# Filler products on TensorE and a reordered start in a state-space and ELU kernel

## The chip, the cores and the metric

The kernel runs on one core of a Trainium2 chip. The metric is device time in microseconds for one execution; before the change the median of seven runs is 390.37 us (389.13 to 390.76).

TensorE is PE in the profile (its weight loads PEld), VectorE DVE, ScalarE ACT, GpSimd POOL, and SyncE, which issues most transfers here, SP.

## The reference

A chunked linear recurrence (Mamba-2) is followed by a two-layer network with an ELU between the layers. All is float32.

```python
for c in range(nc):                       # per batch and head, chunks of the sequence
    cum = np.cumsum(log_a[chunk])         # log_a = log(clip(a, 1e-6, 1))
    M = (C @ B.T) * exp(cum_i - cum_j) * causal
    y = M @ x + (C @ state) * exp(cum)
    state = exp(cum_last) * state + sum_j exp(cum_last - cum_j) * outer(B_j, x_j)
h = y_transposed @ w_in                   # 3072 x 256 by 256 x 2048
g = where(h > 0, h, exp(min(h, 0)) - 1)
out = g @ w_out                           # 3072 x 2048 by 2048 x 256
```

There are 4 batches of 8 heads, a sequence of 768, head size 32 and state size 16. The weights come as 64-bit numbers, and the kernel makes 32-bit ones of them on the chip.

## The kernel before, in words

The sequence is cut into twelve chunks of 256 tokens (chunk `n`, of one batch and all heads). Each chunk has an attention part and then layer 1 and layer 2 of the network. The order of instructions on every engine is that of the program text; nothing is rescheduled. Each engine works its own queue in that order and waits where data or buffers are missing.

The attention part of a chunk is a chain of small products on TensorE with copies and products on the other engines between them:

- `turn` (L369) transposes B and C; ACT copies B out as `bt`, DVE masks C into `ctm` (L382).
- `first_exp` (L349), for the first chunks, spreads exp(cum) over the state rows: a product into `ps_ec`, copied by ACT to `ec`. `turn_exp` (L386) makes `cts` from it on DVE.
- `scaled` (L360) multiplies B by its decay on GpSimd, giving `sc`. `sums` (L481) multiplies `sc` by x into `ps_st`. `states` (L497) carries the state on DVE (`S_new`), and GpSimd masks it into `Sx`.
- `first_decays` (L424) takes four exps of 128x256 on ACT, giving L. `scores` (L451) makes `ps_g`, and `weigh` (L466) makes M = g times L on DVE, in four parts.
- `across` (L523) and `inside` (L543) sum the output in `ps_y`: `across` from the states, `inside` from M and x, in two halves `t`. The halves are copied to `yT`.

`l1(n, i)` (L578) is one of eight steps of layer 1 for a chunk: two groups of 128 hidden columns, each two products of 128x256 in f32, into `ps_h`. `elu` (L594) follows: two instructions on ACT (`e`), one on DVE (`g`). `l2` (L610) is the matching step of layer 2.

The weights come in sixteen pieces, eight of `w_in` and eight of `w_out`. A piece is loaded by `w_load` (on SP's queue), and converted by `w_abs` (ACT, L157), `w_low` (ACT or DVE, L164 or L166), `w_sign` (DVE, L174), `w_high_a` (DVE, the clip of `mag`, L182), `w_high_b` (DVE, L189) and `w_sum` (GpSimd, L199). Step `i` of layer 1 needs piece `i`.

The head of the program (L654 to L746) holds chunks 0 and 1 with the first four steps of layer 1. A first batch of seven idle products (L214, bf16 on zeros, 128x512) stands at the very start of TensorE's queue. The loop at L751 then goes through twelve layer-1 steps of chunks 0 and 1 and the attention of chunk 2. The main loop from L794 alternates one step of layer 2 of chunk n - 2 with one step of layer 1 of chunk n, and places the attention of later chunks between them. `ends` (L786) names the step at which `across` and `inside` of a pair of later chunks are put.

PSUM buffers come from two pools: seven rotating ones (`p_a`, tag `a`), handed out in the order in which they were released, and a single one (`p_o`, tag `o`).

Of the kernel before, what the change touches and what calls it, by code (L numbers as in the profile page):

```python
# [16 lines left out]
P = 128  # L17
# [11 lines left out]
def kernel(  # L29
# [49 lines left out]
    def psum(shape, name):  # L79
        return p_a.tile(shape, F32, tag="a", name=name)  # L80
# [70 lines left out]
    def w_words(i):  # L151
        words = w_raw[i].rearrange("p k (f t) -> p k f t", t=2)
        return words[:, :, :, 0], words[:, :, :, 1]
# [15 lines left out]

    w_sgn = {}  # L170

    def w_sign(i):
        w_sgn[i] = conv.tile([P, 2, CW], U32, tag="sgn", name="sgn")
        nc.vector.tensor_scalar(  # L174
            out=w_sgn[i], in0=w_words(i)[1], scalar1=0x80000000, scalar2=None,
            op0=ALU.bitwise_and)

    def w_high_a(i):
        mag = w_mag[i]


        nc.vector.tensor_scalar(  # L182
            out=mag.bitcast(F32), in0=mag.bitcast(F32),
            scalar1=high_word_as_f32(0x38000000), scalar2=high_word_as_f32(0x47EFFFFF),
            op0=ALU.max, op1=ALU.min)
# [26 lines left out]
    def idle_products(count):  # L212
        for _ in range(count):
            nc.tensor.matmul(  # L214
                out=ps_idle, lhsT=idle, rhs=idle.unsqueeze(1).to_broadcast([P, 4, P]),
                start=True, stop=True)

    idle_products(7)
    ident = const.tile([P, P], F32, name="ident")
# [36 lines left out]
    def make_heads(n):  # L256
# [5 lines left out]

    make_heads(0)
    make_heads(1)
    nc.gpsimd.tensor_scalar(
        out=la, in0=la, scalar1=1e-6, scalar2=1.0, op0=ALU.max, op1=ALU.min)


    def log_of(t):
        nc.scalar.activation(t, t, ACT.Ln)  # L270
# [7 lines left out]
    def to_last(cum, out, eng):  # L278
# [3 lines left out]
            out=out.rearrange("r u (v i) -> r (u v) i", i=Q),  # L282
            in0=cum[:, :, Q - 1:Q].to_broadcast(list(cum.shape)), in1=cum, op=ALU.subtract)

    nc.vector.tensor_scalar(
        out=la0, in0=la0, scalar1=1e-6, scalar2=1.0, op0=ALU.max, op1=ALU.min)
    log_of(la0)
    F0 = const.tile([P, 2, P], F32, name="F0")
    running_sums(la0, F0, P)
# [24 lines left out]
    def turned(src, name, scale, eng):  # L314
        rows = src.shape[0]
        ps = psum([P, 2, rows], "ps_" + name)
        for u in range(2):
            nc.tensor.transpose(out=ps[:, u], in_=src[:, u], identity=ident[0:rows, 0:rows])
        t = const.tile([P, 2, rows], F32, name=name)
        if eng is nc.scalar:  # L320
            eng.copy(out=t, in_=ps)
        else:
            eng.tensor_scalar(out=t, in0=ps, scalar1=scale, scalar2=None, op0=ALU.mult)
        return t
# [23 lines left out]

    def first_exp(n):  # L349

        ps = psum([P, 2, P], "ps_ec") if n else p_o.tile([P, 2, P], F32, tag="o", name="ps_ec")
        rows = slice(BH, 2 * BH) if n < 2 else slice(0, ROWS)
        nc.tensor.matmul(
            out=ps, lhsT=heads[n][rows].rearrange("p h n -> p (h n)"),
            rhs=X0 if n < 2 else F[:, 1], start=True, stop=True,
            tile_position=(rows.start, 0))
        st[n]["ec"] = att.tile([P, 2, P], F32, tag="ec", name="ec", bufs=4)
        nc.scalar.copy(out=st[n]["ec"], in_=ps)
# [10 lines left out]
    def turn(n):  # L369

        s = st[n]
        tb, tc_ = psum([P, 2, P], "ps_tb"), psum([P, 2, P], "ps_tc")
        for k, ps in enumerate((tb, tc_)):
            for u in range(2):
                nc.tensor.transpose(  # L375
                    out=ps[:, u], in_=s["bc"][:, k, u].rearrange("p h n -> p (h n)"),
                    identity=ident)
        s["bt"] = att.tile([P, 2, P], F32, tag="bt", name="bt", bufs=3)
        nc.scalar.copy(out=s["bt"], in_=tb)
        s["ct"] = tc_  # L380
        s["ctm"] = att.tile([P, 2, 2, P], F32, tag="ctm", name="ctm")
        nc.vector.tensor_tensor(  # L382
            out=s["ctm"], in0=tc_.unsqueeze(2).to_broadcast([P, 2, 2, P]),
            in1=hmask2.unsqueeze(1).unsqueeze(3).to_broadcast([P, 2, 2, P]), op=ALU.mult)
# [39 lines left out]
    def first_decays(n, *qs):  # L424

        s = st[n]
        if "L" not in s:
            s["L"] = att.tile([P, NH, 2, Q], F32, tag="L", name="L", bufs=4)
        for q in qs:
            nc.scalar.activation(s["L"][:, 2 * q:2 * q + 2], s["low"][q], ACT.Exp)  # L430
# [20 lines left out]
    def scores(*ns):  # L451

        gs = [psum([P, len(ns), 2, 2, Q], "ps_g") for _ in range(4)]
        for at, n in enumerate(ns):
            s = st[n]
            for u in range(2):
                for v in range(2):
                    for q in range(4):
                        rows, toks = slice(32 * q, 32 * q + 32), slice(Q * v, Q * v + Q)
                        nc.tensor.matmul(  # L460
                            out=gs[q][toks, at, u], lhsT=s["bt"][rows, u, toks],
                            rhs=s["ctm"][rows, u, :, toks], start=True, stop=True,
                            tile_position=(32 * q, Q * v), skip_group_check=True)
            s["g"], s["M"] = [g[:, at] for g in gs], []

    def weigh(n, q):  # L466
        s = st[n]
        M = att.tile([P, 2, 2, Q], F32, tag="M", name="M", bufs=8)
        nc.vector.tensor_tensor(  # L469
            out=M, in0=s["g"][q],  # L470
            in1=s["L"][:, 2 * q:2 * q + 2].rearrange("p k u i -> p u k i"), op=ALU.mult)
        s["M"].append(M)
# [70 lines left out]
    def inside(y, *ns):  # L543


        for t in range(2):
            for at, n in enumerate(ns):
                s = st[n]
                for u in range(2):
                    for v in range(2):  # L550
                        toks = slice(Q * v, Q * v + Q)
                        for q in range(4):
                            h, col = 4 * t + q, (D * q + shift(n, v)) % P
                            nc.tensor.matmul(  # L554
                                out=y[t][v][col:col + D, at, u],
                                lhsT=s["x"][toks, u, D * h:D * (h + 1)],
                                rhs=s["M"][h // 2][toks, u, h % 2], start=False, stop=True,
                                tile_position=(Q * v, col), skip_group_check=True)
            n = ns[0]
            if n // 2 not in yT:  # L560
                yT[n // 2] = ffn.tile([P, KC, 2, 2, P], F32, tag="yT", name="yT")
            out = yT[n // 2][:, t, n % 2:n % 2 + len(ns)]
            for v in range(2):
                k = shift(n, v)
                for at in (0, k) if k else (0,):
                    count, src = P - k, (at + k) % P
                    to, src = out[at:at + count, :, :, Q * v:Q * v + Q], y[t][v][src:src + count]
                    if t and n < 2:
                        nc.vector.tensor_copy(to, src)
                    else:  # L570
                        nc.scalar.copy(out=to, in_=src)  # L571
        for n in ns:
            st.pop(n)
# [88 lines left out]
    first_cum(0)  # L662
    first_decays(0, 0, 1)
    eb0 = turned(E0, "eb0", 1.0, nc.vector)
    turn(0)
    first_exp(0)
    scaled(0, nc.gpsimd)
    first_decays(0, 2, 3)
    turn_exp(0)
    sums(0, parts=(most,))  # L670
    states(0, most)
# [1 line left out]
    w_low(0, nc.scalar)  # L673
    log_of(la)
    scores(0)
    weigh(0, 0)
    weigh(0, 1)
    w_sign(0)
    w_high_a(0)
    w_high_b(0, half[0])  # L680
    w_sum(0, half[0])
    weigh(0, 2)
    weigh(0, 3)
    w_high_b(0, half[1])
    w_sum(0, half[1])
    w_abs(1)
    w_low(1, nc.scalar)
    kept = st[0]
    inside(across(0), 0)

    w_sign(1)
    w_high_a(1)
# [58 lines left out]
    for s, (n, i) in enumerate((  # L751
            (1, 0), (1, 1), (0, 4), (1, 2), (0, 5), (1, 3), (0, 6), (1, 4), (0, 7), (1, 5),
            (1, 6), (1, 7))):
        l1(n, i)
        if s < 8:
            decay_of(2, s)
        if s % 2 == 1 and todo < 10:
            w_take(todo, nc.vector)
            w_give(todo)
            w_load(todo + 6)  # L760
            todo += 1
        if s == 4:
            scaled(2, nc.gpsimd)
        if s == 5:
            turn(2)
            first_exp(2)
            turn_exp(2)
        if s == 7:
            scores(2)
            weigh(2, 0)  # L770
            weigh(2, 1)
        if s == 8:
            spread_cum(3)
            load_x(3)
            spread_exp(3)
            weigh(2, 2)
            weigh(2, 3)
            sums(2, pool=p_o, tag="o")
            states(2)
        if s == 10:  # L780
            inside(across(2), 2)
        if len(lag) > 1:
            elu()


    ends = {(3, 14): 4, (5, 8): 6, (7, 13): 8, (9, 7): 10}  # L786

    def end_of_two(n, step):
        m = ends.get((n, step))
# [101 lines left out]
```

## Time and profile before

| | |
|---|---|
| median of the runs | 390.37 us |
| the profiled execution | 390.84 us |
| its span | 389.0 us |
| mean granted clock of TensorE | 0.991 |
| PE busy | 379.9 us (98%) |
| DVE, ACT, POOL busy | 142.4, 196.5, 74.9 us |
| moved by DMA | 25.24 MB, mean 65 GB/s |
| layer 1 and layer 2 products in the chain that ended last | 41% and 44% of the span |

The page cuts the span into forty slices. Each digit is the busy share of a slice in tenths; the clock row gives the TensorE clock that was granted, in tenths of full speed. The timeline gives the start and the length of an instruction (or of several of one kind, merged, with their number), and in square brackets how long the engine had stood idle and what ended it. An f32 product on TensorE has two records.

### The profile page before, as it was taken

How to read it: one execution, taken by the hardware profiler on the slowest of the kernel's cores; microseconds unless marked ns; L12 is line 12 of the kernel's file. 1: busy time of each engine (PE TensorE's matmuls, PEld its weight loads, DVE VectorE, ACT ScalarE, POOL GpSimd, SP SyncE). 2: the span in 40 equal slices, each digit the busy share in tenths (PEclk: the TensorE clock that was granted, in tenths of full speed). 3: DMA queues.
4: the chain of work that ended last, by engine and by line, in shares of the span. 5: the costliest groups of instructions: out<-in, count | busy, mean ns of one | idle time of the engine just before them, and what ended most of it. 6: DMA issues, size and time to landing. Idle time of an engine off the chain costs nothing.

```text
span 389.0 us, 8711 instructions
## 1 busy us (share of the span) xinstructions
PE 379.9 (98%) x3563; PEld 324.6 (83%) x3563; DVE 142.4 (37%) x288; ACT 196.5 (51%) x456; POOL 74.9 (19%) x135
## 2 busy tenths in 40 slices
PE   7999989999999999999999999999999999999996
PEld 4677778888888888888888888888888888888885
DVE  3979967952521123612223341223432122221000
ACT  4669868776335556353466535367443433334000
POOL 5544534552300022300013120011310000000000
PEclk9699999999999999999999999999999999999999
DMA  8978896455004605003333101540000000000000
GB/s 169 198 180 214 221 210 143 87 82 135 4 0 69 83 14 136 3 3 53 54 57 101 37 2 31 64 71 29 2 3 2 27 2 8 19 2 28 2 27 27
DMA packets 96248, 25.24 MB, mean 65 GB/s; under 512 B 77328, under 2 KB 92112, under 8 KB 96208
## 3 DMA queue, kind: packets, MB, share of 16 engines
q1 hardware_dynamic: 94032, 24.49, 30.2%
q8 instruction: 28, 0.46, 0.5%
q10 hardware_dynamic: 2176, 0.20, 0.4%
q14 instruction: 12, 0.10, 0.1%
HBM read 21.33 MB, written 3.34 MB: 63 GB/s over the span
## 4 chain that ended last, share of the span: by engine, by line
PE 92%; DMA 3%; DVE 2%; issue 1%; SPq 1%; POOL 0%; ACT 0%; ACTq 0%; DVEq 0%
PE ps_h L586 41%; PE ps_o L617 40%; PE ps_o L633 4%; PE ps_y L554 2%; PE ps_g L460 1%; DMA bc<-in_C_dram 1%; PE ps_y L535 1%; PE ps_st L490 1%; DMA flat<-F 1%; PE ps_tb L375 1%; PE ps_tc L375 1%; DMA la<-in_a_dram 1%; DVE M L469 0%; POOL w_in L199 0%; SPq L335 0%
## 5 line engine op out<-in xcount | busy, mean ns | idle before, releaser
L586 PE MATMUL ps_h<-yT,w_in 128*128 128x256 f32 x768 | 183.9, 383 | 1.4 <-issue 0.7
L617 PE MATMUL ps_o<-w_out,g 128*128 128x256 f32 x704 | 166.1, 380 | 0.0
L586 PEld LDWEIGHTS ps_h<-yT,w_in 128*128 128x128 f32 x768 | 145.8, 191 | 23.8 <-issue 2.2
L617 PEld LDWEIGHTS ps_o<-w_out,g 128*128 128x128 f32 x704 | 132.3, 190 | 18.2 <-POOL L L445 0.2
L600 DVE SCALAR_TENSOR_TENSOR g<-e,ps_h 128x512 f32<-128x512 f32 x96 | 65.7, 686 | 205.8 <-ACT e L599 205.7
L598 ACT ACTIVATE e<-ps_h 128x512 f32<-128x512 f32 x96 | 57.1, 595 | 139.9 <-PE ps_h L586 134.3
L599 ACT ACTIVATE e<-e 128x512 f32<-128x512 f32 x96 | 60.5, 630 | 3.1
L445 POOL TENSOR_SCALAR_AFFINE_SELECT L<-L 64x512 f32<-64x512 f32 x40 | 27.5, 686 | 159.7 <-ACT L L440 158.3
L440 ACT ACTIVATE L<-L,ncum 128x64 f32<-128x64 f32 x160 | 42.0, 332 | 0.0
L571 ACT COPY yT<-ps_y 64x256 f32<-64x256 f32 (+3 forms) x41 | 13.2, 324 | 10.8 <-PE ps_y L554 10.4
L469 DVE TENSOR_TENSOR M<-ps_g,L 128x256 f32<-128x256 f32 x48 | 17.0, 414 | 0.2
L512 POOL TENSOR_TENSOR Sx<-S_new,hmask 128x64 f32<-128x64 f32 x44 | 12.8, 302 | 16.9 <-DVE S_new L507 11.9
L623 ACT COPY ob<-ps_o 128x512 f32<-128x512 f32 x11 | 6.4, 578 | 15.3 <-PE ps_o L617 15.3
L633 PE MATMUL ps_o<-w_out,g 128*128 128x256 f32 x64 | 14.0, 379 | 0.0
L199 POOL TENSOR_TENSOR w_in<-mag,w_in 128x512 uint32<-128x512 uint32 (+1 forms) x9 | 11.0, 1223 | 14.7 <-DVE mag L189 9.8
L633 PEld LDWEIGHTS ps_o<-w_out,g 128*128 128x128 f32 x64 | 12.2, 190 | 1.7
L199 POOL TENSOR_TENSOR w_out<-mag,w_out 128x512 uint32<-128x512 uint32 x8 | 10.2, 1273 | 15.0 <-DVE mag L189 13.1
L189 DVE SCALAR_TENSOR_TENSOR mag<-mag,sgn 128x512 uint32<-128x512 uint32 (+1 forms) x17 | 12.0, 707 | 0.6
L157 ACT ACTIVATE mag<-w 128x512 f32<-128x512 f32 x16 | 10.8, 673 | 1.9 <-POOL w_in L199 1.0
L507 DVE SCALAR_TENSOR_TENSOR S_new<-S_new,ec,ps_st 128x64 f32<-128x64 f32 x40 | 10.9, 279 | 2.0
L554 PE MATMUL ps_y<-M,xr 64*32 64x64 f32 x768 | 10.4, 232 | 0.4 <-DVE M L469 0.4
L554 PEld LDWEIGHTS ps_y<-M,xr 64*32 64x32 f32 x768 | 8.6, 109 | 1.4 <-DVE M L469 0.7
(73 smaller groups left out, 140.0 us busy)
## 6 DMA issues: line engine op xcount, KB each, us to landing
L<-flat SPq DMA_DIRECT2D x20, 256.0 KB, 5.0
w<-in_moe_w_in_dram SPq DMA_DIRECT2D x8, 512.0 KB, 5.2
w<-in_moe_w_out_dram SPq DMA_DIRECT2D x8, 512.0 KB, 6.6
xr<-in_x_dram SPq DMA_DIRECT2D x24, 128.0 KB, 3.3
out_dram<-ob SPq DMA_DIRECT2D x11, 256.0 KB, 2.2
bc<-in_B_dram SPq DMA_DIRECT2D x24, 64.0 KB, 3.7
bc<-in_C_dram SPq DMA_DIRECT2D x22, 64.0 KB, 2.9
ec<-flat_exp SPq DMA_DIRECT2D x72, 16.0 KB, 1.7
```

What stands on the lines that cost most here:

```text
L199: nc.gpsimd.tensor_tensor(out=w, in0=w_mag[i][:, :, cols], in1=w, op=ALU.add)
L440: nc.scalar.activation(L[:, h, u], L[:, h, u], ACT.Exp, bias=ncum[:, u, row:row + 1])
L445: nc.gpsimd.affine_select(out=part, in_=part, pattern=[[0, 4], [0, 2], [1, Q]], compare_op=ALU.is_ge, fill=0.0, base=0, channel_multiplier=-1)
L469: nc.vector.tensor_tensor(out=M, in0=s["g"][q], in1=s["L"][:, 2 * q:2 * q + 2].rearrange("p k u i -> p u k i"), op=ALU.mult)
L554: nc.tensor.matmul(out=y[t][v][col:col + D, at, u], lhsT=s["x"][toks, u, D * h:D * (h + 1)], rhs=s["M"][h // 2][toks, u, h % 2], start=Fal ...
L571: nc.scalar.copy(out=to, in_=src)
L586: nc.tensor.matmul(out=ps[:, j], lhsT=w_in[:, k, m * P:(m + 1) * P], rhs=yT[n // 2][:, k, n % 2].rearrange("p u i -> p (u i)"), start=(k = ...
L598: nc.scalar.activation(e, ps, ACT.Relu, scale=-1.0)
L599: nc.scalar.activation(e, e, ACT.Exp, scale=-1.0)
L600: nc.vector.scalar_tensor_tensor(out=g_of[n][:, 2 * i:2 * i + 2], in0=e, scalar=1.0, in1=ps, op0=ALU.subtract, op1=ALU.max)
L617: nc.tensor.matmul(out=o_of[n][:, ts], lhsT=g_of[n][:, m, ts * P:(ts + 1) * P], rhs=w_out[:, m], start=(m == 0 and ts == 0), stop=(m == MC ...
L633: nc.tensor.matmul(out=ps, lhsT=g_of[n][:, m, ts * P:(ts + 1) * P], rhs=w_out[:, m], start=(m == 0), stop=(m == MC - 1))
```

## The change

- `idle_product(k)` is new: one product of the f32 identity by k copies of itself, into the idle PSUM tile, which nobody reads. It stands with k = 3 (384 columns) after `scores(0)` and after `inside(across(0), 0)`. One bf16 idle product stands between the two halves of `inside` for chunk 0. The idle tile stays in `p_o` longer for this, and `ps_ec` of chunk 0 takes a buffer of `p_a`.
- `w_sign` and `w_high_a` can do half of a piece's columns; for piece 0 sign, clip, high word and sum now go half by half, and two of the `weigh` stand earlier among them.
- The clip of `la` goes from GpSimd to DVE, ahead of `turn(0)`.
- The last two exps of `first_decays(0, ...)` go ahead of `first_exp(0)` (on ACT ahead of the copy of `ec`).
- Both halves of `yT` of chunk 0 are copied by ACT (one by DVE before), and `w_low(1)` on ACT goes behind them.
- In the loop of twelve steps, `scores(2)` and the first two `weigh(2, ...)` go ahead of the conversion of the weight piece in the same step. On TensorE this changes no order; on DVE two M go ahead of the four instructions of the conversion.
- In `ends`, the last pair's `across` and `inside` go from step 7 to step 6 of chunk 9, ahead of one layer-1 step.

SP's queue keeps its order.

```diff
-    def w_sign(i):
-        w_sgn[i] = conv.tile([P, 2, CW], U32, tag="sgn", name="sgn")
+    def w_sign(i, cols=slice(None)):
+        if i not in w_sgn:
+            w_sgn[i] = conv.tile([P, 2, CW], U32, tag="sgn", name="sgn")
         nc.vector.tensor_scalar(
-            out=w_sgn[i], in0=w_words(i)[1], scalar1=0x80000000, scalar2=None,
-            op0=ALU.bitwise_and)
-
-    def w_high_a(i):
-        mag = w_mag[i]
+            out=w_sgn[i][:, :, cols], in0=w_words(i)[1][:, :, cols], scalar1=0x80000000,
+            scalar2=None, op0=ALU.bitwise_and)
+
+    def w_high_a(i, cols=slice(None)):
+        mag = w_mag[i][:, :, cols]
...
+    def idle_product(k):
+
+        nc.tensor.matmul(
+            out=ps_idle[:, 0:k], lhsT=ident, rhs=ident.unsqueeze(1).to_broadcast([P, k, P]),
+            start=True, stop=True)
...
-    nc.gpsimd.tensor_scalar(
-        out=la, in0=la, scalar1=1e-6, scalar2=1.0, op0=ALU.max, op1=ALU.min)
+    def clip(t):
+        nc.vector.tensor_scalar(
+            out=t, in0=t, scalar1=1e-6, scalar2=1.0, op0=ALU.max, op1=ALU.min)
...
-        ps = psum([P, 2, P], "ps_ec") if n else p_o.tile([P, 2, P], F32, tag="o", name="ps_ec")
+        ps = psum([P, 2, P], "ps_ec")
...
         for t in range(2):
+            if t and ns[0] == 0:
+                idle_products(1)
             for at, n in enumerate(ns):
...
-                    if t and n < 2:
+                    if t and n == 1:
                         nc.vector.tensor_copy(to, src)
                     else:
                         nc.scalar.copy(out=to, in_=src)
...
     eb0 = turned(E0, "eb0", 1.0, nc.vector)
+    clip(la)
     turn(0)
+    first_decays(0, 2, 3)
     first_exp(0)
     scaled(0, nc.gpsimd)
-    first_decays(0, 2, 3)
     turn_exp(0)
...
     scores(0)
+    idle_product(3)
     weigh(0, 0)
     weigh(0, 1)
-    w_sign(0)
-    w_high_a(0)
+    w_sign(0, half[0])
+    w_high_a(0, half[0])
+    weigh(0, 2)
+    weigh(0, 3)
     w_high_b(0, half[0])
     w_sum(0, half[0])
-    weigh(0, 2)
-    weigh(0, 3)
+    w_sign(0, half[1])
+    w_high_a(0, half[1])
     w_high_b(0, half[1])
     w_sum(0, half[1])
     w_abs(1)
-    w_low(1, nc.scalar)
     kept = st[0]
     inside(across(0), 0)
+    idle_product(3)
+    w_low(1, nc.scalar)
...
         l1(n, i)
         if s < 8:
             decay_of(2, s)
+        if s == 7:
+            scores(2)
+            weigh(2, 0)
+            weigh(2, 1)
         if s % 2 == 1 and todo < 10:
             w_take(todo, nc.vector)
             w_give(todo)
...
-        if s == 7:
-            scores(2)
-            weigh(2, 0)
-            weigh(2, 1)
...
-    ends = {(3, 14): 4, (5, 8): 6, (7, 13): 8, (9, 7): 10}
+    ends = {(3, 14): 4, (5, 8): 6, (7, 13): 8, (9, 6): 10}
```

## The prediction

> **What bounds the kernel now.** I read the page's busy shares first (PE 98% of the span), then its slices, then the stretch ahead of the first layer microsecond by microsecond. In the slices a full PE row says nothing of its clock; the clock row has one hole, in the second slice.
>
> ```profile
> PE   7999989999999999999999999999999999999996
> ...
> PEclk9699999999999999999999999999999999999999
> ```
>
> The windows of one microsecond (columns: stretch, length, PE, PEld, DVE, ACT, POOL busy, granted clock, DMA share, GB/s) show the holes and then the price:
>
> ```profile
> 8.00:9.00 1.00, 0.23 (x24) 0.24 (x24) 0.43 (x2) 0.81 (x3) 0.63 (x2) 1.00 1.03 332
> 9.00:10.00 1.00, 0.82 (x56) 0.48 (x36) 0.62 (x3) 0.53 (x1) 0.37 (x2) 1.00 0.97 363
> 10.00:11.00 1.00, 0.72 (x24) 0.71 (x24) 1.00 (x4) 1.00 (x3) 0.52 (x2) 0.77 0.93 256
> 11.00:12.00 1.00, 0.90 (x44) 0.54 (x36) 0.97 (x4) 0.82 (x3) 0.00 (x0) 0.50 1.09 330
> 14.00:17.00 3.00, 3.00 (x9) 2.19 (x8) 2.97 (x6) 1.28 (x2) 1.60 (x1) 0.50 0.74 146
> 17.00:18.00 1.00, 1.00 (x29) 0.66 (x34) 0.96 (x2) 0.88 (x2) 0.29 (x1) 0.81 1.23 298
> ```
>
> The clock is 0.50 from about 10.8 (0.77 in its microsecond) to about 17.4 (0.81). The timeline of PE shows who pays:
>
> ```profile
> 8.77 0.43 PE L490 MATMUL ps_st<-xr,sc 64*32 64x64 f32 x24 [0.93 <-POOL sc L365]
> 9.12 0.69 PE L460 MATMUL ps_g<-ctm,bt 32*64 32x128 f32 x32
> 10.28 1.02 PE L535 MATMUL ps_y<-cts,Sx 32*64 32x64 f32 x24 [0.46 <-POOL Sx L512]
> 11.22 0.68 PE L554 MATMUL ps_y<-M,xr 64*32 64x64 f32 x32
> 12.35 1.00 PE L554 MATMUL ps_y<-M,xr 64*32 64x64 f32 x32 [0.44 <-DVE M L469]
> 13.27 3.78 PE L586 MATMUL ps_h<-yT,w_in 128*128 128x256 f32 x8
> 18.92 1.99 PE L586 MATMUL ps_h<-yT,w_in 128*128 128x256 f32 x8
> ```
>
> The same eight records take 3.78 us at 13.27 and 1.99 at 18.92. Behind 29 us a second limit stands: from 29 to 54 DVE is busy 23.9 of 25 us and the DMA share is 0.91. After 56 the waits of PE list nothing, and the last 333 us are dense: what is won by 56 is won at the end.
>
> [...] a mag clip on DVE takes 0.42, but 1.48 beside a GpSimd sum, which itself takes 1.89 in place of 1.28.
>
> **The change, part by part**
>
> ```profile
> 6.94 1.07 POOL L265 TENSOR_SCALAR la<-la 96x256 f32<-96x256 f32 x1 [1.71 <-DMA la<-in_a_dram]
> 8.09 0.62 POOL L365 TENSOR_TENSOR sc<-bc,eb 128x256 f32<-128x256 f32 x1
> ...
> 10.75 0.42 DVE L174 TENSOR_SCALAR sgn<-w 128x512 uint32<-128x512 uint32 x1
> ...
> 11.88 0.75 DVE L469 TENSOR_TENSOR M<-ps_g,L 128x256 f32<-128x256 f32 x2
> ```
>
> 1. The clip of la leaves GpSimd (1.07 us) for DVE, where its twin on la0 takes 0.29. The sc product then starts behind it at about 7.3, not 8.09. Queued behind the clip on DVE is ctm, which starts at 7.32; la lands at 2.78 + 4.0 = 6.8, so the clip ends near 7.25 and costs ctm at most 0.1. A later la would hold ctm, and the scores on PE, one for one. x has landed (7.1 and 7.8), so the sums of chunk 0 start at 7.95, not 8.77.
>
> 2. ps_ec takes a rotating PSUM buffer, so its product waits for a first exp (over by 7.2), and two more exps go ahead of the ec copy on ACT. They issue about 0.27 apart: ec from 7.87 to about 8.0, cts from 8.28 to 8.43. The scores now wait for buffers that those exps and ec release, about 8.4. They start there, not at 9.12. First S_new 9.31 to 8.85, first M 10.08 to 9.6.
>
> 3. By halves: between the second and third M stand a full sgn (0.34 from start to start), a full clip (0.4) and half of the high word (0.35); after the change, two halves of about 0.2. Third M from 11.88 to 10.7, where the clip needs w_abs(0), done at 10.14. The first half's sum on GpSimd (0.72) ends at 12.5, not 12.83; the second at 13.4, not 13.91. DVE has two more instructions, about 0.1.
>
> 4. yT's second half of chunk 0 goes to ACT, and w_low(1) behind it. ACT is over with w_abs(1) at 11.96 (w landed at 11.2), copies four times by 12.7, then does w_low(1) by 13.45, in time for piece 1's sum at 14.0, which waits for DVE. DVE saves 0.49.
>
> 5. The fillers. A 256-column f32 product takes 1.73/4 = 0.43 us at full clock and 3.72/4 = 0.93 at half, so 384 columns cost 0.65 or 1.39. The one after the scores runs 9.05 to 9.7, while PE would wait for Sx (about 9.75): free. [...] The last runs from 11.8 to 12.5, when the first half-weight (12.5) and yT (12.3, 12.7) come: free at full clock, 1.39 on the path at half.
>
> 6. The clock. From 7.4 to 10.8 PE is now filled some 3.3 of 3.4 us. I take it that the clock holds. Then layer 1 starts at 12.6, not 13.27 (-0.7); its four products take 1.8, not 3.58 (-1.8); the low and cum products behind it run at full clock (-0.3). Second layer-1 step at 16.1, not 18.92: -2.8. Piece 1 is ready by about 15.5 to 15.9.
>
> 7. What takes some of it back. Piece 3 lands at 14.29 + 3.9 = 18.2; ACT's w_abs(3), at 20.08 before, can move by 1.9 only, and bt and ec of chunk 1 stand behind it: about -2.1 at the end of inside(1). Then piece 6: its issue (29.58) follows SP's queue and not PE, and it lands at 34.1. ACT takes it at 35.54, DVE at 35.96, so these move by 1.4 and 1.8: I take -1.6.
>
> 8. M ahead of weights.
>
> ```profile
> 45.09 0.85 DVE L166 TENSOR_SCALAR w_out<-w 128x512 f32<-128x512 uint32 x1
> ...
> 47.73 0.75 DVE L469 TENSOR_TENSOR M<-ps_g,L 128x256 f32<-128x256 f32 x2
> ...
> 48.21 0.46 PE L490 MATMUL ps_st<-xr,sc 64*32 64x64 f32 x32 [0.93 <-DVE M L469]
> ...
> 53.95 0.92 PE L586 MATMUL ps_h<-yT,w_in 128*128 128x256 f32 x3 [0.40 <-DVE g L600]
> ```
>
> PE's wait of 0.93 goes, since M follows the scores (45.33) at once. But DVE has no gap from 45.09 to 53.9, and layer 1 at 53.95 waits for its g: PE only waits longer there. What DVE itself gains: w_low and sgn took 0.85 and 0.89 in place of 0.42 beside GpSimd's mask of L (45.00 to 46.48), and M (0.41 beside GpSimd too) now stands there: about 0.5, less 0.2 of waiting for the scores: -0.3.
>
> 9. In the last pair inside goes one layer-1 step ahead: 284.6, not 286.46. Its last Sx ends at 284.62, and PE needs it some 0.2 into the step: 0, with 0.2 lost if Sx is late.
>
> Sum: -1.6 - 0.3 = -1.9. The profiled execution took 390.84 with a span of 389.0: 387.1 and 388.9. It stands 0.47 above the median of 390.37; from the median, 388.5.
>
> **Rivals**
>
> - *The clock is lost for one window only* (10.8 to 14.2): the last filler ends at 13.9, layer 1 runs mostly at full clock, second step at 17.6, -1.3; pieces 3 and 6 are no limit then. With -0.3: 388.8 to 389.5. [...] Against it: the fillers leave hardly a gap.
> - *Nothing is taken back*: other waits give way with PE, -2.8 to -3.5: 386.9 to 387.6. Against it: the landings in 7 follow the DMA queue.
> - *It doesn't do what it says, or the gain dies in DVE*: the clock falls as before, or the saturated stretch from 29 to 54 gives all back: 390.0 to 390.6. For it: that stretch, and that small tiles kept the records of 11 to 13 busy without bringing the clock back.
> - *Slower*: the last filler stands in series at half clock. If the clock falls at 10.8 and M comes no earlier than before, inside ends at 13.35, the filler adds 1.39 and a weight load of 0.2, layer 1 starts at 14.9, +1.6; with -0.3, 391.7. It decides once inside ends after 12.6 - 1.4 = 11.2 with a clock at half. Against it: M comes a microsecond earlier by 3[...].
>
> **How the numbers follow.** Forecast 0.50 (its own range 387.6 to 389.3), one window 0.15, nothing taken back 0.10, no gain 0.17, slower 0.08. Predicted 388.5. From 387.0 to 390.6 it leaves out the slower case and half of the best one. A measurement here tells 0.2%, 0.8 us, from no change: faster is below 389.6. Forecast, best, and most of one window: 0.70; slower 0.10; the rest 0.20.
>
> **What would show it.** Right: clock 1.00 from 10 to 18; layer 1's first step near 12.6 and 1.9 long; second near 16.1; sc near 7.3; no wait of ps_st for M near 47; a longer wait before layer 1 at 53. ACT or DVE waiting for piece 3 or 6 shows step 7 right. Wrong: half clock anywhere behind 10; layer 1 starting after 13.3 right behind a filler; a wait of DVE for la ahead of ctm; a wait of PE for Sx at 283.

## The result, and the profile after

The changed kernel took **387.28 us** as the median of 12 runs (386.72 to 388.44). The kernel before took 390.21 (31 runs, the first seven among them). The ratio is 0.9933, with a 95% interval from 0.9915 to 0.9951: 2.6 us less by the ratio, 2.9 by the medians. The forecast was 388.5, which is 1.9 less than before; the measured time lies just below the range of its main case (387.6 to 389.3). The profiled execution took 386.88 with a span of 385.0, against 390.84 and 389.0, so between the two profiles lie 4.0 us. One disturbed execution of 491.98 us, of the kernel wait_for_g below, is left out of its median.

The page of the changed kernel has no hole in the clock row. The second slice of PE, a 9 before as well, says nothing of it.

```profile
PE   8999999999999999999999999999999999999996
...
PEclk9999999999999999999999999999999999999999
```

The windows of the start, same columns as in the prediction, show where the work was put. PE was busy 0.23 us of the microsecond from 8 to 9 before, and now it is busy for all of it.

```profile
8.00:9.00 1.00, 1.00 (x57) 0.71 (x37) 0.62 (x4) 0.34 (x2) 0.00 (x0) 1.00 1.02 352
...
10.00:11.00 1.00, 1.00 (x57) 0.69 (x53) 1.00 (x5) 0.87 (x2) 0.00 (x0) 1.00 0.93 270
11.00:12.00 1.00, 1.00 (x34) 0.71 (x34) 1.00 (x4) 0.92 (x4) 0.24 (x1) 1.00 1.16 259
14.00:17.00 3.00, 2.89 (x57) 2.13 (x57) 2.97 (x5) 2.75 (x6) 1.90 (x1) 1.00 0.91 215
```

The timeline of the changed kernel, most of PE's records with the first product of sc on GpSimd and the first M on DVE, shows the start of layer 1:

```profile
7.07 0.62 POOL L372 TENSOR_TENSOR sc<-bc,eb 128x256 f32<-128x256 f32 x1 [1.82 <-DVE eb L330]
7.78 0.43 PE L497 MATMUL ps_st<-xr,sc 64*32 64x64 f32 x24
8.17 0.90 PE L467 MATMUL ps_g<-ctm,bt 32*64 32x128 f32 x32
9.00 0.91 PE L221 MATMUL ps_idle<-ident 128*128 128x384 f32 x2
9.47 0.75 DVE L476 TENSOR_TENSOR M<-ps_g,L 128x256 f32<-128x256 f32 x2
10.76 0.39 PE L215 MATMUL ps_idle<-idle 128*128 128x512 bf16 x1
11.71 0.91 PE L221 MATMUL ps_idle<-ident 128*128 128x384 f32 x2
12.66 1.13 PE L595 MATMUL ps_h<-yT,w_in 128*128 128x256 f32 x4
14.11 1.13 PE L595 MATMUL ps_h<-yT,w_in 128*128 128x256 f32 x4 [0.32 <-POOL w_in L200]
15.08 0.60 PE L407 MATMUL ps_x<-low,ident 128*128 128x256 bf16 x4
16.92 1.99 PE L595 MATMUL ps_h<-yT,w_in 128*128 128x256 f32 x8
```

The first layer-1 step starts at 12.66 (13.27 before), takes 2.42 to the low products (3.58 before), and these with the cum products take 1.84 (2.07 before). The second step therefore starts at 16.92 in place of 18.92: 0.61 + 1.16 + 0.23 = 2.0.

Later on, the timeline of the changed kernel answers the prediction's lines at 48.21 and 53.95:

```profile
45.49 0.45 PE L497 MATMUL ps_st<-xr,sc 64*32 64x64 f32 x32
45.88 3.72 PE L595 MATMUL ps_h<-yT,w_in 128*128 128x256 f32 x16
...
49.94 0.88 PE L563 MATMUL ps_y<-M,xr 64*32 64x64 f32 x64
50.98 1.99 PE L595 MATMUL ps_h<-yT,w_in 128*128 128x256 f32 x8
52.81 1.89 PE L626 MATMUL ps_o<-w_out,g 128*128 128x256 f32 x8
```

Three waits of PE have gone between the scores of chunk 2 and the first layer-2 step: 0.93 for M, 0.40 for g ahead of step (1,7), and one that the prediction did not show, inside that step. Here it is in the timeline of the kernel before:

```profile
55.58 1.24 PE L586 MATMUL ps_h<-yT,w_in 128*128 128x256 f32 x5 [0.72 <-issue]
```

The gain place by place, in the two profiles:

| Work on PE | before | after | gain so far |
|---|---|---|---|
| first layer-1 step | 13.27 | 12.66 | 0.6 |
| second layer-1 step | 18.92 | 16.92 | 2.0 |
| across of chunk 1 | 26.96 | 25.17 | 1.8 |
| scores of chunk 2 | 44.64 | 42.92 | 1.7 |
| sums of chunk 2 | 48.21 | 45.49 | 2.7 |
| layer-1 step (1,7) | 53.95 | 50.98 | 3.0 |
| first layer-2 step | 56.66 | 52.81 | 3.85 |
| end of the span | 389.0 | 385.0 | 4.0 |

So two places pay: the start (1.7 at the scores) and the stretch around M of chunk 2 (2.1 more). For the second the prediction had 0.3. The profiles also exaggerate: the one of before stands 0.6 above its median, the one of after 0.4 below. The experiments had to say why step (1,7) of layer 1 (chunk 1, step 7) waits for nothing now, and what a gap put down to "issue" is, one for which the profile shows no releaser.

### The profile page after: what moved, and what is told of

Read it like the earlier page. It is cut to its first block, busy times and chain, and to the rows that moved or that the text cites. A ratio compares the mean times of both kernels' runs of the same rounds, so it can differ in the third digit from the quotient of the medians.

```text
span 385.0 us, 8722 instructions
## 1 busy us (share of the span) xinstructions
PE 379.3 (99%) x3568; PEld 323.8 (84%) x3568; DVE 142.6 (37%) x289; ACT 196.8 (51%) x458; POOL 73.9 (19%) x134
## 4 chain that ended last, share of the span: by engine, by line
PE 95%; DVE 2%; ACT 1%; POOL 1%; DMA 1%; issue 0%; ACTq 0%; DVEq 0%
PE ps_h L595 43%; PE ps_o L626 40%; PE ps_o L642 4%; PE ps_y L563 2%; PE ps_g L467 2%; PE ps_y L542 1%; PE ps_st L497 1%; PE ps_tb L382 1%; PE ps_tc L382 1%; POOL w_in L200 1%; DMA la<-in_a_dram 1%; DVE mag L190 0%; DVE M L476 0%; PE ps_x L418 0%; PE ps_x L426 0%
## 5 line engine op out<-in xcount | busy, mean ns | idle before, releaser
L595 PE MATMUL ps_h<-yT,w_in 128*128 128x256 f32 x768 | 181.9, 381 | 1.0 <-POOL w_in L200 0.7
L580 ACT COPY yT<-ps_y 64x256 f32<-64x256 f32 (+3 forms) x43 | 13.5, 323 | 11.7 <-PE ps_y L563 11.2
L157 ACT ACTIVATE mag<-w 128x512 f32<-128x512 f32 x16 | 10.8, 673 | 1.9 <-DMA w<-in_moe_w_in_dram 1.1
L514 DVE SCALAR_TENSOR_TENSOR S_new<-S_new,ec,ps_st 128x64 f32<-128x64 f32 x40 | 10.9, 278 | 2.0
L183 DVE TENSOR_SCALAR mag<-mag 128x512 f32<-128x512 f32 (+1 forms) x17 | 10.3, 606 | 1.1 <-ACT mag L157 1.1
```

Source lines behind the costliest of these rows:

```text
L595: nc.tensor.matmul(out=ps[:, j], lhsT=w_in[:, k, m * P:(m + 1) * P], rhs=yT[n // 2][:, k, n % 2].rearrange("p u i -> p (u i)"), start=(k = ...
```

## The experiments

Each is compared with the kernel before, which ran beside it: 390.6, 390.2 and 390.3 us by the medians on the three chips used. Where a second kernel is named, it is by the medians, often across chips, so differences of a few tenths say little.

**M of chunk 2 moved alone, and everything except it.** The two edits are complements.

```
m_alone: the kernel before, in the loop over steps
             decay_of(2, s)
+        if s == 7:
+            scores(2)
+            weigh(2, 0)
+            weigh(2, 1)
         if s % 2 == 1 and todo < 10:
...
-        if s == 7:
-            scores(2)
-            weigh(2, 0)
-            weigh(2, 1)

all_but_m: the changed kernel with this move undone
```

> The kernel before with one part of the change alone: the scores of chunk 2 and the first two M ahead of the weight piece on DVE. Theory (the two traces): this part is worth about 2 us by itself, because the layer-1 step (1,7) no longer takes the PSUM buffer that DVE's g releases but one that ACT's copy to yT releases: some 2 us below the kernel before, the wait of ps_st for M gone, (1,7) starting right behind the products of inside(2), half clock from about 10.5 to 17.4 as before. Rival (the prediction's step 8): DVE has no gap there, so PE only waits longer ahead of (1,7): 0.3 us below the kernel before.

Measured: 388.6 (387.5 to 390.02), ratio 0.9956 [0.9942, 0.997]. PE's timeline of this kernel:

```profile
47.41 0.45 PE L490 MATMUL ps_st<-xr,sc 64*32 64x64 f32 x32
...
51.87 0.88 PE L554 MATMUL ps_y<-M,xr 64*32 64x64 f32 x64
52.70 1.99 PE L586 MATMUL ps_h<-yT,w_in 128*128 128x256 f32 x8
54.53 1.89 PE L617 MATMUL ps_o<-w_out,g 128*128 128x256 f32 x8
```

The start is that of before, half clock included (6.83 us of it in both). Yet the first layer-2 step comes at 54.53, not 56.66: the move alone brings 2.1 in the profile and 0.44%, or 1.7, in the times. DVE's g of the step before ends at 53.67 here (52.99 + 0.68), while (1,7) starts at 52.70: it cannot have waited for that g.

> The changed kernel with that part alone undone (M of chunk 2 behind the weight piece again). Theory: about 2 us above the changed kernel, with PE waiting 0.9 for M at the sums of chunk 2 and waiting for g ahead of (1,7); the start up to 42 us as in the changed kernel. Rival (step 8): 0.3 above it.

Measured: 389.67 (388.95 to 393.04), ratio 1.0008 [0.9986, 1.003]: with M late the whole of the new start is worth nothing that the ratio can tell from zero (by the medians of its own chip 0.9 is left). PE's timeline:

```profile
47.58 0.46 PE L497 MATMUL ps_st<-xr,sc 64*32 64x64 f32 x32 [0.91 <-DVE M L476]
...
52.03 0.89 PE L563 MATMUL ps_y<-M,xr 64*32 64x64 f32 x64
54.94 3.68 PE L595 MATMUL ps_h<-yT,w_in 128*128 128x256 f32 x8 [2.02 <-issue]
```

and its clock, in a window over that step:

```profile
55.00:58.50 3.50, 3.50 (x9) 2.80 (x10) 2.50 (x6) 2.14 (x4) 0.00 (x0) 0.51 0.11 33
```

The wait for M is back (0.91), and ahead of (1,7) PE stands for 2.02 us with no releaser; the g of step (0,7) ends at 53.26, so at most the first 0.34 of it can be the wait for g. At its end the clock falls to half for 3.41 us, and the step takes 3.68, not 1.99. This profile was 0.6 us ahead of the one of before at the sums of chunk 2 (47.58 against 48.21), and loses that and more here. It is not the usual case: it took 392.68, another execution 393.04, each with a mean clock of about 0.994, while the other twelve of the 14 kept 0.999 or more and have a median of 389.6. What these lose against the changed kernel, some 2.3, no profile shows. The half-clock stretches within these profiles are 3.41 us long (this one, no_fillers, two in changed_shifted) or 6.83, twice that (before, m_alone). The prediction's "one window" is a stretch of 3.41 us.

**Why (1,7) no longer waits for g.** Each layer-1 step takes a PSUM buffer in turn, and when it may start depends on who releases the one it gets. In the built program, the first product of (1,7) waits in the kernel before for DVE, whose g of step (0,7) frees that PSUM buffer. In the changed kernel it waits for ACT: the buffer was last that of the first half of inside for chunk 2, which ACT's copy into yT frees. It is so in the build of m_alone too, and DVE again in all_but_m. The move leaves the order in which buffers are asked for (m_alone asks as the kernel before does); what it changes is the order of DVE's work, which releases buffers, and (1,7) is given another one. The trace of the changed kernel agrees: ACT's copies ran, and (1,7) started before that g did.

```profile
50.46 1.66 ACT L580 COPY yT<-ps_y 128x128 f32<-128x128 f32 x6 [2.67 <-PE ps_y L563]
50.98 1.99 PE L595 MATMUL ps_h<-yT,w_in 128*128 128x256 f32 x8
51.07 0.68 DVE L609 SCALAR_TENSOR_TENSOR g<-e,ps_h 128x512 f32<-128x512 f32 x1
```

In the profile of m0_before_piece_again (below), the wait for ACT can be seen itself, and again (1,7) starts before the g of (0,7) ends (52.18):

```profile
51.50 0.68 DVE L609 SCALAR_TENSOR_TENSOR g<-e,ps_h 128x512 f32<-128x512 f32 x1
51.91 1.99 PE L595 MATMUL ps_h<-yT,w_in 128*128 128x256 f32 x8 [0.69 <-ACT yT L580]
```

What the wait is worth was tried by putting it back with other means: a product of eight columns that reads the last part of that g, and whose result the step overwrites.

```
wait_for_g: the changed kernel, in l1, ahead of the step's products
+        if (n, i) == (1, 7):
+            nc.tensor.matmul(
+                out=ps[:, 0, 0:8], lhsT=g_of[0][:, 14, 0:P], rhs=ident[:, 0:8],
+                start=True, stop=True)
```

> The changed kernel with one tiny product (8 columns, overwritten at once) ahead of layer-1 step (1,7) that reads the g of step (0,7): it puts back the wait for DVE that the other PSUM buffer had removed, and nothing else; its two weight loads cost up to 0.4 us. Theory (the buffer is a part of the gain): (1,7) starts right behind that g, 0.8 us later than in the changed kernel, and the time is 0.8 to 1.2 above it. Rival (the buffer is no matter, PE had time there anyway): within 0.4 of the changed kernel.

Measured: 388.47 (387.94 to 389.06), ratio 0.9963 [0.9949, 0.9977]. That is 1.2 above the changed kernel, by the ratios too, and 1.1 above the kernel without the last filler (387.38), which ran beside it. No profile of it can be read. In the changed kernel g ends at 51.75 and (1,7) starts at 50.98: the wait costs 0.8 as it stands, and the times show 0.3 to 0.4 more, which stays unexplained (the added product brings its own instructions to PE as well). The wait for g was a real part of the price that the move took away; step 8 had left it standing, and longer.

**The fillers.** Away from the changed kernel, and put alone into the kernel before:

```
no_fillers: the changed kernel
-            if t and ns[0] == 0:
-                idle_products(1)
...
     scores(0)
-    idle_product(3)
...
     inside(across(0), 0)
-    idle_product(3)

fillers_alone: the kernel before, with these three and with
+        ps = psum([P, 2, P], "ps_ec")
```

> The changed kernel without its three filler products. Theory: the fillers hold the clock; without them a stretch of 6.8 us at half clock comes back near 10.5, the second layer-1 step starts 1 to 2 us later, and the time is 1.0 to 1.8 above the changed kernel. Rival: the closer order alone holds the clock and the fillers do nothing: clock 1.00 throughout and the time within 0.3 of the changed kernel.

Measured: 388.78 (386.55 to 390.36), ratio 0.9953 [0.9936, 0.997]: above the changed kernel by 1.5 by the medians and by 0.8 by the ratios, whose intervals overlap. In its profile the clock was half for 3.41 us, from 14.88 to 18.29, and layer 1 ran in it. PE's and ACT's timelines:

```profile
12.53 0.78 PE L561 MATMUL ps_y<-M,xr 64*32 64x64 f32 x32 [1.54 <-DVE M L476]
...
14.18 3.27 PE L593 MATMUL ps_h<-yT,w_in 128*128 128x256 f32 x8 [0.88 <-POOL w_in L200]
```

```profile
11.15 0.66 ACT L157 ACTIVATE mag<-w 128x512 f32<-128x512 f32 x1 [2.65 <-DMA w<-in_moe_w_in_dram]
```

Part of this profile is no matter of fillers: the first weight piece came late (ACT took it at 11.15, against 9.24 in the changed kernel's profile). How much of this profile's loss is the late piece stays open.

The mean granted clock of every execution says more than one profile. 3.41 us at half take 3.41 x 0.5 / 386 = 0.004 off the mean, and 6.83 take 0.009: the profile of no_fillers has 3.41 and 0.996, that of before 6.83 and 0.991. All 12 executions of the changed kernel kept 0.999 or more; without the fillers 3 of 22 did, and of the kernel before 6 of 61 on the same chip as no_fillers. The three have a median of 387.5, near the changed kernel; ten with a mean clock of 0.994 to 0.996 have 388.3, nine with 0.991 have 389.6. So in this order of the start the fillers keep the clock (12 of 12 against 3 of 22), and losing it goes with about a microsecond for each 3.41 us at half. A late piece may be a part of this too, since the executions were sorted by their clock after the fact.

> The kernel before with the three filler products alone (and the PSUM buffer of ps_ec that they need). Theory: the clock holds, layer 1 starts no later than 13.3 and runs at full clock, the second step near 17; 1.2 to 1.8 us below the kernel before. Rival: the old order leaves holes enough (1.0 at the sums) for the clock to fall all the same, the last filler then stands in series, and the time is 0 to 1 us above the kernel before.

Measured: 390.77 (389.48 to 394.99), ratio 1.0025 [0.9999, 1.0051]: no gain, where 1.2 to 1.8 were expected. In the profile the clock held to the end, but the first layer-1 step began later than before (13.88, not by 13.3), and further on a gap stood in PE's timeline:

```profile
13.88 1.98 PE L594 MATMUL ps_h<-yT,w_in 128*128 128x256 f32 x8
17.50 1.99 PE L594 MATMUL ps_h<-yT,w_in 128*128 128x256 f32 x8
...
51.30 0.87 PE L562 MATMUL ps_y<-M,xr 64*32 64x64 f32 x63
53.09 0.21 PE L562 MATMUL ps_y<-M,xr 64*32 64x64 f32 x1 [0.93 <-issue]
```

The second step at 17.50 is 1.4 earlier than before. A gap of 0.93 put down to issue has appeared at 52.16, and another of 0.69 at 288.49. Of the 17 executions, 11 kept a clock of 0.999 or more (median 390.2) and 6 did not (392.2 and more): with the fillers alone the clock is not kept every time (where it fell, no profile shows), and where it is kept the time is hardly better than before (390.6).

**Fillers and M together, without the rest of the start.** This is the kernel before with both edits above.

> The kernel before with two parts of the change: the fillers, and M of chunk 2 ahead of the weight piece. Theory (the start's new order, without the fillers, was worth nothing: 388.8 against 388.6 for M alone; the fillers hold the clock): 387.2 to 387.8, as the changed kernel. Rival (the fillers need the new order, since in the old one they made the kernel 1 us slower): 388.5 or above, layer 1 later than 13.5.

Measured: 388.0 (387.62 to 388.62), ratio 0.9946 [0.9926, 0.9965]. The clock held, layer 1 began at 13.38, and one gap stood in its first step:

```profile
13.38 0.81 PE L594 MATMUL ps_h<-yT,w_in 128*128 128x256 f32 x3
15.13 1.24 PE L594 MATMUL ps_h<-yT,w_in 128*128 128x256 f32 x5 [0.94 <-issue]
```

By medians the three fillers add 0.6 to the move of M, and the new order of the start (clip, exps, halves, yT) 0.6 again: 388.6, 388.0, 387.4 (the changed kernel beside it). The second of these steps is shown: both kernels ran on one chip, and every run of fillers_and_m (387.62 to 388.62) lies above every run of the changed kernel there (387.13 to 387.54). The first is not: by the ratios it is 0.4, inside the intervals and across chips. Without the fillers the new order gives nothing: no_fillers 388.8, m_alone 388.6, on one chip.

**The last filler alone.**

```
no_last_filler: the changed kernel
     inside(across(0), 0)
-    idle_product(3)
     w_low(1, nc.scalar)
```

> The changed kernel without the last filler alone (the one between inside(0) and layer 1). Theory: [...] the last stands in a wait for the first half of the weight piece and is free either way: clock 1.00, within 0.3 of the changed kernel. Rival: it is the one that keeps the clock, and without it a stretch at half clock comes back: 0.8 to 1.5 above. Second rival: it delays layer 1, and without it the time is 0.3 to 0.6 below.

Measured: 387.38 (386.67 to 388.1), ratio 0.9931 [0.9906, 0.9955]: the changed kernel's time. PE's timeline:

```profile
12.96 2.57 PE L595 MATMUL ps_h<-yT,w_in 128*128 128x256 f32 x8 [0.87 <-POOL w_in L200]
```

Where the filler stood, PE now waits 0.87 for GpSimd's sum of the first half, and the clock holds all the same. The filler fills a wait that is there anyway; it costs nothing that can be measured and is not needed: all six executions kept a clock of 0.999 or more. The first two fillers are enough.

**M of chunk 0 ahead of the first weight piece.** The changed kernel is put a step further, so that the last two M of chunk 0 do not stand behind the piece's sign and clip on DVE.

```
m0_before_piece: the changed kernel
     weigh(0, 1)
+    weigh(0, 2)
+    weigh(0, 3)
     w_sign(0, half[0])
     w_high_a(0, half[0])
-    weigh(0, 2)
-    weigh(0, 3)
```

> The changed kernel with the last two M of chunk 0 ahead of the first weight piece's sign and clip on DVE. Theory (the first piece lands anywhere from 9.2 to 11.2 in the profiles so far, and DVE stands on it with M behind): inside(0) no longer waits for M when the piece is late; layer 1 starts 0.6 later when it is early and 0.6 earlier when it is late; the time is within 0.5 of the changed kernel, with less spread between runs. Rival: the start sets the end, and 0.6 later on DVE shows as 0.6 above the changed kernel.

Measured: 386.97 (386.48 to 387.51), ratio 0.9918 [0.9893, 0.9943]. That looked 0.3 better than the changed kernel, so both were run again on one chip.

> The changed kernel with the last two M of chunk 0 ahead of the first weight piece, once more beside the changed kernel. Theory (it is free of the first piece's landing): 0.2 to 0.5 us below the changed kernel of this call. Rival: no difference, within 0.2.

Measured: 387.36, ratio 0.9927 [0.9904, 0.9949].

> The changed kernel once more, beside the others of this call: ratio to the kernel before 0.991 to 0.995, no gap put down to issue on PE. It is the measure for the other three.

Measured: 387.39 (387.13 to 387.54), ratio 0.9926 [0.9902, 0.995]. There is no difference, nor less spread (386.71 to 387.86 against 387.13 to 387.54). In both profiles with M ahead, layer 1 waits 0.4 for GpSimd's sum of the weight piece, and not for M. No version here is shown to beat the changed kernel.

The repeat of the changed kernel had an issue gap after all, in its first layer-1 step, and a span of 385.6:

```profile
12.90 1.13 PE L595 MATMUL ps_h<-yT,w_in 128*128 128x256 f32 x4
15.21 1.13 PE L595 MATMUL ps_h<-yT,w_in 128*128 128x256 f32 x4 [1.18 <-issue]
```

**Where the issue gaps stand.** The page lists a queue that no line of the kernel uses, the same in both kernels:

```profile
q8 instruction: 28, 0.46, 0.5%
```

These are 28 transfers of 16384 bytes. Set beside the gaps, each gap without a releaser (of 0.7 us or more) ends 1.3 to 1.7 us after the end of such a transfer; three of them:

| Kernel | gap | transfer ended | to the gap's end |
|---|---|---|---|
| before | 54.86 to 55.58 | 54.06 | 1.52 |
| all_but_m | 52.92 to 54.94 | 53.32 | 1.62 |
| fillers_alone | 52.16 to 53.09 | 51.68 | 1.41 |

They also stand near the same places of PE's instruction order: in step (1,7) or just ahead of it in all three, about the 722nd to 724th product. The fillers put more instructions ahead, and the gap moved back by some products of the kernel. If a gap belongs to a place in the count of PE's instructions, and not to a step of the kernel, more instructions ahead shift every such place. The test cuts the seven idle products at the very start into 28 of a quarter of the columns, 42 instructions more on PE (a load and a product each) and no more columns:

```
m_late_shifted: all_but_m, changed_shifted: the changed kernel
-    idle_products(7)
+    for _ in range(28):
+        nc.tensor.matmul(out=ps_idle[:, 0], lhsT=idle, rhs=idle, start=True, stop=True)
```

> The changed kernel with M of chunk 2 late again, and the seven idle products of 512 columns at the very start cut into 28 of 128 columns: the same idle time, 42 more instructions on PE. Theory (the gap near 53 to 55, put down to issue, sits at a fixed place in PE's instruction stream[...]): the gap moves 21 products earlier, to about the 43rd of the 64 records of M by x in inside(2), and ends some 1.5 us after the instruction transfer on queue 8 that starts at 50 to 52.5. Rival (the gap belongs to that step of the kernel, a hidden wait): it stays just ahead of or inside layer-1 step (1,7).

Measured: 401.5 (400.41 to 401.6), ratio 1.0287 [1.0256, 1.0317], 11.8 above all_but_m (10.9 by the ratios). The place foreseen for the gap near 53 was missed: there is none in inside for chunk 2 now. In its stead others stand along the run, 8.7 us in sum. Two of them in PE's timeline, and PE's waits for the page's "issue" (sum, times, longest):

```profile
13.88 0.34 PE L565 MATMUL ps_y<-M,xr 64*32 64x64 f32 x15 [2.17 <-issue]
...
244.42 0.24 PE L565 MATMUL ps_y<-M,xr 64*32 64x64 f32 x1 [1.64 <-issue]
```

```profile
PE ps_y L565 <- issue: 7.8, 5, 2.2
```

> The changed kernel with its seven idle products of 512 columns cut into 28 of 128 columns (the same idle time, 42 more instructions on PE). Theory (gaps come [...] within a burst of small products, and end 1.3 to 1.6 us after an instruction transfer on queue 8): the same gaps as with M late, inside(0), inside(1) and four of the later pairs, some 8 us in sum, and 9 to 12 us above the changed kernel. Rival (the gaps there came from M being late): within 1 us of the changed kernel.

Measured: 400.13 (397.83 to 401.62), ratio 1.0249 [1.021, 1.0288], 12.7 above the changed kernel. Its waits of PE:

```profile
PE ps_y L565 <- issue: 8.3, 5, 2.0
PE ps_h L597 <- issue: 1.4, 1, 1.4
```

The gaps make up 9.7 of the 12.4 us between its span and that of the changed kernel; two stretches of half clock, 3.41 us each (29.72 to 33.13, 173.08 to 176.49; the mean clock is 0.991), can make up the rest. In both kernels the gaps end 1.3 to 1.7 us after a transfer, and stand in the bursts of small products (five of the six here write ps_y), where PE starts the most instructions per microsecond (64 records in 0.88 us at 49.94 in the changed kernel, 8 in 1.99 for step (1,7) behind them).

Counting all of PE's products from the start, the places agree. Both shifted kernels stand after the products 220, 473, 1481, 1987, 2620 and 3126, though 21 of these are now idle ones and the work there is other work than before; the gaps of the unshifted kernels lie after 219 or 220 (fillers_and_m, changed_again), after 722 to 724 (the table) and after 3125 (fillers_alone). The distances (253, 1008, 506, 633, 506) are whole multiples of 126 to 127 products. Between the last three transfers of the profiles before and after, PE starts 254 to 258 loads and products from one to the next, between the others 38 to 502, and the 7227 records of PE's queue in the changed kernel, waits included, make 258 for each of the 28. So there is about one transfer for twice the 126 to 127 products (a load with each) whose multiples separate the gaps.

What the shift shows is that the gaps follow the count of instructions: the same work with 42 more ahead of it takes 3% longer. What PE stands for there is not shown: the gaps agree with these counts and with the times of the transfers, and no run changes the transfers. Most transfers pass without a gap: of the 28 in the profile of the kernel before, one is followed by a gap of 0.7 us or more, and of the 28 in that of the changed kernel, none.

Not tried: the clip, the exps, the halves and yT's copies singly; the last pair's move singly; another PSUM buffer for (1,7) with M left where it was. Why the transfer near 52 comes later with M late stays open: it ended 5.74 us after the start of the sums of chunk 2 in all_but_m, 5.85 in the kernel before, and 4.0 in the changed kernel, 3.35 in m_alone.

## Why the prediction was right in sign and short in size

Steps 1 to 5 held, most of their starts to 0.2 us. The sc product started at 7.07 (7.3 predicted), the sums at 7.78 (7.95), the scores at 8.17 (8.4), the first M at 9.47 (9.6), the third at 10.54 (10.7). ctm started at 7.33 in place of 7.32. The f32 fillers took some 0.9 and not 0.65, the bf16 one 0.39 (the seven at the very start took 0.43 each). The last was free nevertheless: no_last_filler shows its place as a wait. For the other two no run shows it.

Step 6 was right about the clock and too large in size. From 7.4 to 10.8 PE was busy for all of the 3.40 us (2.01 before), the clock held for the whole run, and the first layer-1 step started at 12.66 (12.6). But the step took 2.42 and not 1.8: its second half waited 0.32 at 14.11 for GpSimd's sum. Step 3 had put the end of that sum at 13.4, and it came at 13.81: DVE's second high word took 0.83 (12.06), beside GpSimd's first sum, against 0.41 for the first (11.20), and each sum took 0.85 and not 0.72. The seam between the halves cost about as much again (2.42 less 1.8 and 0.32). Behind it the low and cum products won 0.23 and not 0.3. So the second step moved by 2.0, not 2.8. One reason was overrated: in all_but_m and fillers_alone the held clock and the earlier second step bring no gain that the ratios show; in their profiles a later gap gives it back.

The reading of the clock was a little off. A mean of 0.77 from 10 to 11 is 0.54 us at full and 0.46 at half, so the clock fell at 10.54, not 10.8, and stayed at half for 6.83 us. In the 3.41 us ahead of the fall, from 7.13, PE's records fill 2.02, in the 3.41 ahead of these 2.67; the sums of the step don't change. That the filling of these 3.4 us decides over the clock was the author's assumption; the runs show how often it was kept: in 12 of 12 executions of the changed kernel, 12 of 14 of all_but_m, 11 of 17 of fillers_alone, and 3 of 22 of no_fillers.

Step 7 came to the right number by a reason that is not shown. The scores of chunk 2 moved by 1.7, near the predicted 1.6. ACT took piece 3 at 18.05 and piece 6 at 33.82, earlier by 2.0 and 1.7; the step had 1.9 and 1.4. Piece 6 was issued as late as before (29.64, before 29.58), and yet ACT took it ahead of the 34.1 at which the step let it land. Its evidence was to be ACT or DVE waiting for these pieces, and in the waits of ACT between 10 and 50 us the only wait for a weight transfer is one of 0.2, ahead of piece 1; DVE waits for neither piece:

```profile
ACT mag L157 <- POOL w_in L200: 0.8, 1, 0.8
...
ACT mag L157 <- DMA w<-in_moe_w_in_dram: 0.2, 1, 0.2
```

Piece 3 was also issued earlier, at 13.57 and not 14.29; the step had held its issue fixed. What limited the stretch was the slower second half of the first layer-1 step, which had taken 0.8 of the 2.8 before any landing could.

Step 8 failed. It said that DVE has no gap from 45.09 to 53.9, that step (1,7) waits for DVE's g, and that PE therefore only waits longer there: 0.3. From the scores of chunk 2 to the first layer-2 step PE took 12.02 us before, 9.89 after and 9.69 in m_alone: 2.1 to 2.3 in the profiles, 1.7 by the times of m_alone. Two things stood against it. First, the wait for g was no matter of the data, which step (1,7) doesn't read, but of the PSUM buffer, and which one is given follows from the order in which buffers are released. Moving M ahead changed DVE's order, and with it the buffer and the engine for which (1,7) waits. The page's wait "for DVE g" was true of the kernel before and was carried over to a build where it is no longer so. The waits in the changed build would have told, and they hang on no run. Second, the 0.72 inside (1,7) was in the trace of before and was not counted; that the move takes it away in most executions is not shown, since a gap of this kind comes and goes (1.18 in changed_again, none in the first profile of the same kernel).

Step 9 fits: in the last pair across starts at 280.88 and PE waits for no Sx. No run has this move alone.

The sum came out near because two errors went opposite ways: 0.3 was foreseen around M and about 1.7 is there by the times, while of the 1.6 foreseen for the start the changed kernel keeps 1.2 on top of M (388.6 against 387.4), and without M's move little or nothing. That the time lies within 387.0 to 390.6 is in part luck: the larger of the two gains came where the prediction saw almost none. Of the rivals, one window lost and no gain fell, since the clock was kept in all 12 executions, and the slower one fell with the clock: nothing stood in series at half clock. "Nothing is taken back" named the right size, 386.9 to 387.6, for a wrong reason: 0.8 and 0.3 of the start were lost on the way in the profile, and the stretch around M made up for it.

## What to carry to other kernels

A wait named in the profile as "for g" can be a wait for the buffer that g frees (here the 0.40 ahead of (1,7)); where a change moves any work that asks for or releases a rotating buffer, look up in the changed build which engine each critical step now waits for, before carrying an old wait over. Count gaps without a releaser on the bounding engine (0.7 to 2.2 us each here) as part of the price, and judge an edit at the start by what the end keeps: a gain won early can be given back at a later gap, as the profiles of all_but_m (2.02) and fillers_alone (0.93, 0.69) show. Look at the clock of every execution and not of the profiled one alone.

## What the runs showed of the hardware that was not expected

- PE stood without a releaser at places that follow the count of its instructions. The gaps were 0.7 to 2.2 us long, ended 1.3 to 1.7 us after a 16 KB instruction transfer, lay at whole multiples of 126 to 127 products from each other, and mostly in or behind runs of small products. 42 more instructions at the start, for the same idle columns, cost 11.8 and 12.7 us in two kernels.
- At the end of the gap of 2.02 us in all_but_m the clock fell to half for 3.41 us.
- The clock fell with no long gap too: the longest ahead of the fall at 10.54 in the kernel before is 0.93. In the 3.41 us up to a fall PE's records fill 2.02 us in the kernel before, 1.5 in no_fillers (11.47 to 14.88) and 1.4 in all_but_m (51.53 to 54.94). In the kernel before, 3.41 us filled to 2.67 stand ahead of its 2.02 at full clock. Behind the fall come 3.41 us filled to 2.97 and 3.42 filled to the end, all at half, and then full clock.
- With the first two fillers, some 1.3 us of products (0.91 and 0.39), the changed kernel without the third kept a mean clock of 0.999 or more in all six executions.
- The first weight piece is taken by ACT between 9.0 and 11.2 us in the profiles of these kernels, and with the new order the two latest (10.7 in all_but_m, 11.15 in no_fillers) go with the two latest starts of layer 1 (13.71 and 14.18, against 12.66), the shifted kernels apart.
